# Mask and row maximum in two wide VectorE steps, and a first piece of the MLP set among the attention blocks

## Chip, cores and metric

The kernel runs on one core of a Trainium2 chip. The metric is device time in microseconds. Engines are named as in the profile: PE is TensorE's matmul (PEld its weight load), DVE is VectorE, ACT is ScalarE, POOL is GpSimd, SP is SyncE, which issues most of the DMAs.

## What is computed

Windowed softmax attention, a Fourier mixing with a layer norm and an MLP, and a gated MLP, chained, for 4 batches of 576 tokens with 8 heads of 64 (512 features):

```
rel = pos[:, None] - pos[None, :]
scores = where((rel >= 0) & (rel < 64), q @ k.T / 8, -1e9)
x = softmax(scores) @ v                      # [4, 576, 512]
u = x + real(fft(fft(x, axis=1), axis=2))
u = u + relu(layernorm(u) @ w_ch1) @ w_ch2   # hidden width 2048
h = gelu_tanh(u @ w_in);  a, v = split(h)
v = w_sg @ (layernorm(v) * g_ln) + b_sg      # along the tokens
out = u + (a * v) @ w_out
```

## The kernel before

**Order of the work.** `emit` writes the program as generators that `drive` interleaves: a main generator yields costs, and each lane beside it is advanced by as much. A scheduler then fixes, by its own model, in which order each engine takes the instructions; that order is static on the chip. The stages are the attention, the MLP over 2048 hidden columns, the gated MLP. Beside the attention run lane `weights` (decoding of the weights of FF tiles 0 to 2, `decode`, L144 to L161) and lane `work` (`dft` and `ln` of chunk 0 and of chunk 1).

**Attention.** 36 blocks n (batch b, 64 queries j). `scores` (L254) multiplies the block's queries with 128 keys for four pairs of heads into one PSUM tile `sc` of 4 x 128 columns. For each pair one VectorE step `tensor_tensor_reduce` (L264; in the trace CUSTOM_DVE_ANT_0 and a DVE_READ_ACCUMULATOR2_ANT behind it) adds the mask, writes `s` and the row maximum `mx`; ScalarE takes the exponential of the four pairs (L268). `transposes` (L272) transposes `s` over PSUM tile `pt` into `pts`, `pv` (L281) multiplies with the values, `norm` (L293) divides, `xt` (L312) transposes the result over PSUM tile `xt` into `uT`, which holds all tokens with features on partitions. They follow their block by 1, 2 and 3 blocks (`LAG`). `load_attn` issues the loads of block n + 4 on SP: q in a ring of three, k in three buffers (three blocks each), v in three buffers (two blocks each). The Fourier tables come in four DMAs on POOL's queue, written at blocks 2, 4, 7 and 9 (`TAB_AT`, L376); nothing in them waits for a block. The mask is loaded behind block 0's q and k (L327).

**Fourier step.** `dft(b)` (L380) folds `uT` of a batch: O on GpSimd (L389), E on VectorE (L390), both folded on VectorE (L393, L405), split into high and low parts; a one-row sum `gr`/`grow` on VectorE (L401, L402, L404). Then products with the tables. `ln(n)` (L487) normalises a chunk of tokens into `xh[n]` and `xl[n]`.

**MLP.** A batch's tokens are two chunks of 320 and 256, eight in all; HEAD is chunks 0 to 3, TAIL 4 to 7. `PHASES` lists which FF tiles f go over which chunks, in order. For each (f, chunk): 12 products into `h` (4 x `mm3`, three products each for high and low parts), relu on ScalarE (`rh`, L568), rest on VectorE (`rl`, L569), two tiles later 12 products into `acc` (`second`, L535); behind the last tile of a phase four VectorE adds bring `acc` into `uT` (L549). Beside it run `rest` (decoding of tile 3, `ln` of chunks 2 and 3 with `dft(2)`, `dft(3)`, `ln` of TAIL) and further decodings.

## Time and profile before

| | |
|---|---|
| runs shown | 816.88 us median of 3 (815.56 to 817.01) |
| the profiled execution | 811.93 us |
| its span (first to last instruction) | 810.2 us |
| busy: PE, PEld, DVE, ACT, POOL | 777.8, 748.4, 478.2, 290.9, 163.5 us |
| chain that ended last, by engine | PE 74%, DVE 14%, DMA 6%, ACT 2%, issue 2% |

PE and PEld overlap, and a matmul's end in the trace is modelled, so start-to-start times tell more of TensorE's pace than durations do. In the chain, "DMA" is a wait for a transfer and "issue" time in which the engine waited for nothing that is shown.

### The profile page before, as it was taken

What the parts mean: (1) busy time and instruction counts of PE and PEld (TensorE: products, weight loads), DVE (VectorE), ACT (ScalarE), POOL (GpSimd) and SP (SyncE); (2) the same over time, 40 slices, a digit from 0 to 9 for tenths busy, and PEclk for the clock granted to TensorE, in tenths of its full rate; (3) what the DMA queues carried; (4) which work ended last, traced back from release to release, by engine and by line L of the source; (5) the groups of instructions that cost most, each with busy time, mean ns of one, the idle gap of its engine ahead of it and who ended that gap; (6) DMA issues with size and microseconds to landing.
All of it is one profiled execution on the core that took longest, in us unless ns stands there. A gap on an engine that the chain in (4) does not pass through costs nothing.

```text
span 810.2 us, 15611 instructions
## 1 busy us (share of the span) xinstructions
PE 777.8 (96%) x6084; PEld 748.4 (92%) x6084; DVE 478.2 (59%) x1390; ACT 290.9 (36%) x710; POOL 163.5 (20%) x202
## 2 busy tenths in 40 slices
PE   5979798899999999999999999999999999999998
PEld 5779597899998999999999999999999998989898
DVE  2688978996488557963226933643240258565653
ACT  3777776442233234431113411333242243131310
POOL 1143513442031013410002300232260021010100
PEclk8999999999999999999999999999999999999999
DMA  9997631121012003420002400132140020303032
GB/s 208 295 323 224 177 97 38 61 97 53 2 40 66 1 1 105 129 82 1 1 2 69 136 6 1 34 118 85 40 134 12 0 60 1 117 1 118 1 117 93
DMA packets 59321, 63.70 MB, mean 79 GB/s; under 512 B 22384, under 2 KB 42736, under 8 KB 59248
## 3 DMA queue, kind: packets, MB, share of 16 engines
q1 hardware_dynamic: 58672, 59.75, 24.9%
q0 software_dynamic: 576, 2.97, 1.2%
q8 instruction: 48, 0.79, 0.4%
q14 instruction: 25, 0.20, 0.1%
HBM read 53.25 MB, written 9.44 MB: 77 GB/s over the span
## 4 chain that ended last, share of the span: by engine, by line
PE 74%; DVE 14%; DMA 6%; ACT 2%; issue 2%; SPq 1%; POOL 1%; DVEq 0%; ACTq 0%
PE acc L118 7%; PE acc L119 7%; PE acc L120 7%; PE h L119 6%; PE h L120 6%; PE h L118 6%; PE c L119 6%; PE c L118 6%; PE c L120 6%; PE g L118 3%; PE g L119 3%; PE g L120 3%; DMA dec_s<-in_w 2%; PE sc L260 2%; DMA dec_s<-in_wo 2%
## 5 line engine op out<-in xcount | busy, mean ns | idle before, releaser
L118 PE MATMUL acc<-rh,set 128*128 128x256 f32 (+1 forms) x512 | 151.6, 296 | 2.2 <-DVE uT L549 2.1
L118 PE MATMUL h<-xh,set 128*128 128x256 f32 (+1 forms) x512 | 151.2, 296 | 0.8 <-DVE rl L569 0.8
L119 PE MATMUL acc<-rl,set 128*128 128x256 f32 (+1 forms) x512 | 151.3, 296 | 0.0
L120 PE MATMUL acc<-rh,set 128*128 128x256 f32 (+1 forms) x512 | 151.1, 295 | 0.0
L119 PE MATMUL h<-xl,set 128*128 128x256 f32 (+1 forms) x512 | 151.0, 295 | 0.0
L120 PE MATMUL h<-xh,set 128*128 128x256 f32 (+1 forms) x512 | 150.9, 295 | 0.0
L569 DVE SCALAR_TENSOR_TENSOR rl<-h,rh 128x320 fp32r<-128x320 f32 (+1 forms) x128 | 58.1, 454 | 118.1 <-ACT rh L568 117.6
L160 POOL TENSOR_TENSOR set<-dec_w,set 128x256 fp32r<-128x256 f32 x88 | 71.9, 823 | 253.7 <-ACT set L159 250.4
L568 ACT ACTIVATE rh<-h 128x320 fp32r<-128x320 f32 (+1 forms) x128 | 51.7, 404 | 161.2 <-PE h L120 121.3
L118 PEld LDWEIGHTS acc<-rh,set 128*128 128x128 f32 x512 | 96.4, 188 | 3.6 <-issue 1.3
L118 PEld LDWEIGHTS h<-xh,set 128*128 128x128 f32 x512 | 96.3, 188 | 1.7 <-DVE rl L569 1.3
L120 PEld LDWEIGHTS acc<-rh,set 128*128 128x128 f32 x512 | 96.5, 188 | 0.1
L119 PEld LDWEIGHTS h<-xl,set 128*128 128x128 f32 x512 | 96.4, 188 | 0.1
L120 PEld LDWEIGHTS h<-xh,set 128*128 128x128 f32 x512 | 96.4, 188 | 0.0
L119 PEld LDWEIGHTS acc<-rl,set 128*128 128x128 f32 x512 | 96.4, 188 | 0.0
L549 DVE TENSOR_TENSOR uT<-acc,uT 128x320 f32<-128x320 f32 (+1 forms) x160 | 62.0, 448 | 15.2 <-PE acc L120 15.2
L154 ACT ACTIVATE dec_g<-dec_s 128x256 f32<-128x256 f32 x88 | 38.4, 438 | 78.6 <-DVE dec_w L156 37.0
L268 ACT ACTIVATE s<-s,mx 128x128 f32<-128x128 f32 x144 | 46.9, 393 | 26.4 <-DVE mx L264 26.3
L482 POOL TENSOR_TENSOR rq<-rq,mhalf 128x1 f32<-128x1 f32 (+2 forms) x26 | 17.4, 669 | 189.9 <-DVE rq L481 186.8
L155 DVE TENSOR_SCALAR dec_w<-dec_s 128x256 int32<-128x256 int32 x88 | 34.8, 398 | 35.3 <-POOL set L160 23.1
L120 PE MATMUL c<-xh,set 128*128 128x256 f32 (+1 forms) x188 | 55.4, 294 | 0.0
L118 PE MATMUL c<-xh,set 128*128 128x256 f32 (+1 forms) x188 | 55.3, 294 | 0.0
(190 smaller groups left out, 1611.9 us busy)
## 6 DMA issues: line engine op xcount, KB each, us to landing
dec_s<-in_w SPq DMA_DIRECT2D x64, 256.0 KB, 2.8
v<-in_v SPq DMA_DIRECT2D x16, 520.0 KB, 6.0
k<-in_k SPq DMA_DIRECT2D x11, 512.0 KB, 6.5
dec_s<-in_wi SPq DMA_DIRECT2D x16, 256.0 KB, 2.8
q<-in_q SPq DMA_DIRECT2D x30, 128.0 KB, 5.4
x<-uT SPq DMA_DIRECT2D x4, 640.0 KB, 3.9
out<-uT SPq DMA_DIRECT2D x4, 640.0 KB, 3.9
dec_s<-in_wo SPq DMA_DIRECT2D x8, 256.0 KB, 2.5
```

Of the source, the lines that this page charges most:

```text
L118: mm(out, lhsT=lh, rhs=rh, start=first and i == 0, stop=False)
L119: mm(out, lhsT=lh, rhs=rl, start=False, stop=False)
L120: mm(out, lhsT=ll, rhs=rh, start=False, stop=last and i == n - 1)
L154: nc.scalar.activation(out=g, in_=s[:, :, 1].bitcast(F32), func=AF.Copy, scale=2.0 ** -112)
L155: nc.vector.tensor_scalar(out=w, in0=s[:, :, 0], scalar1=29, scalar2=None, op0=ALU.logical_shift_right)
L160: (eng or nc.gpsimd).tensor_tensor(out=lo[:, o:o + 256], in0=f, in1=hi[:, o:o + 256], op=ALU.subtract)
L260: nc.tensor.matmul(sc[:, hp], lhsT=q[:, hp].rearrange("p a b -> p (a b)"), rhs=k[:, hp, o:o + 128], start=True, stop=True)
L268: nc.scalar.activation(out=s[:, hp], in_=s[:, hp], func=AF.Exp, bias=mx[:, hp:hp + 1], scale=-1.0)
L482: self.nc.gpsimd.tensor_tensor(out=y, in0=v, in1=self.mhalf[:m, 0:n], op=ALU.pow)
L549: V.tensor_tensor(out=x, in0=acc[:, c, 0:size], in1=x, op=ALU.add)
L568: A.activation(out=rh, in_=o, func=AF.Relu)
L569: V.scalar_tensor_tensor(out=rl, in0=o, scalar=0.0, in1=rh, op0=ALU.max, op1=ALU.subtract)
```

## The change

- `scores`: one `scalar_tensor_tensor` over 512 columns scales and masks, one `tensor_reduce` over the same 512 takes four negated maxima.
- `sc`, `pt` and `xt` share one PSUM ring of three (before: two, one and one); the bank left over is the new tile `e`.
- `dft`: O goes to VectorE behind E; the three `gr`/`grow` steps go to GpSimd.
- `load_tables` first copies four columns of the last block's `mx` into the table's place on GpSimd, so that each table DMA waits for its block. The mask is loaded between the two halves of the first k.
- k and v have two buffers each; v is loaded one block later (`VL` 3).
- `early`: hidden tiles 0 to 2 of chunk 0 (320 rows) and their way into `uT` as a lane beside the attention, once `ln(0)` and the decoding of tiles 0 to 2 have been written. Chunk 0 later takes tiles 3 to 5 behind chunks 1 to 3.

```diff
+E0 = range(3)
-PHASES = [(range(P0), HEAD), (range(P0, 6), HEAD), (range(P0), TAIL), (range(P0, 6), TAIL),
+PHASES = [(range(P0), HEAD[1:]), (range(3, 6), HEAD[:1]), (range(P0, 6), HEAD[1:]), (range(P0), TAIL), (range(P0, 6), TAIL),
-VL = 2
+VL = 3
-UB, SB, QB, VB = 3, 3, 3, 3
+UB, SB, QB, VB = 3, 3, 3, 2
@@ load_k
-        t = self.ap_.tile([128, 4, 256], F32, tag="k", bufs=3, name="k")
+        t = self.ap_.tile([128, 4, 256], F32, tag="k", bufs=2, name="k")
             self.nc.sync.dma_start(t[:, :, c], self.aps["k"][b, :, :, o + c.start:o + c.stop])
+            if b == g == c.start == 0:
+                self.nc.sync.dma_start(self.mask, self.aps["mask"])
@@ scores
-            sc = ps.tile([128, 4, 128], F32, tag="sc", bufs=2, name="sc")
+            sc = ps.tile([128, 4, 128], F32, tag="ab", bufs=3, name="sc")
+            nc.vector.scalar_tensor_tensor(
+                out=s, in0=sc, scalar=0.125, in1=self.mask[:, int(j == 0)].unsqueeze(1).to_broadcast([128, 4, 128]),
+                op0=ALU.mult, op1=ALU.add)
+            nc.vector.tensor_reduce(out=mx, in_=s, axis=AX.X, op=ALU.max, negate=True)
             for hp in range(4):
-                nc.vector.tensor_tensor_reduce(
-                    out=s[:, hp], in0=sc[:, hp], in1=self.mask[:, int(j == 0)], scale=-0.125, scalar=3e38,
-                    op0=ALU.add, op1=ALU.min, accum_out=mx[:, hp:hp + 1])
-            for hp in range(4):
-                nc.scalar.activation(out=s[:, hp], in_=s[:, hp], func=AF.Exp, bias=mx[:, hp:hp + 1], scale=-1.0)
-            st[n] = s
+                nc.scalar.activation(out=s[:, hp], in_=s[:, hp], func=AF.Exp, bias=mx[:, hp:hp + 1])
+            st[n], st['mx'] = s, mx
@@ transposes, xt
-            pt = ps.tile([128, 4, 128], F32, tag="pt", bufs=1 + XPT, name="pt")
+            pt = ps.tile([128, 4, 128], F32, tag="ab", bufs=3, name="pt")
...
+            t = ps.tile([128, 4, 128], F32, tag="ab", bufs=3, name="xt")
@@ load_tables
+        self.nc.gpsimd.tensor_copy(self.tab[:, c.start:c.start + 4], after[:, 0:4])
         self.tc.keep_in_program_order(self.nc.gpsimd.dma_start(self.tab[:, c], self.aps["tab"][:, c]))
@@ dft
-        G.tensor_tensor(out=O, in0=x[:, 0:2], in1=x[:, 2:4], op=ALU.subtract)
         EF.tensor_tensor(out=E, in0=x[:, 0:2], in1=x[:, 2:4], op=ALU.add)
+        EF.tensor_tensor(out=O, in0=x[:, 0:2], in1=x[:, 2:4], op=ALU.subtract)
...
-        V.tensor_copy(gr[:, 0:1], O[0:1, 0, 0:1])
-        V.tensor_tensor(out=gr[:, 1:289], in0=O[0:1, 0, 1:289], in1=O[0:1, 0, 575:287:-1], op=ALU.add)
+        G.tensor_copy(gr[:, 0:1], O[0:1, 0, 0:1])
+        G.tensor_tensor(out=gr[:, 1:289], in0=O[0:1, 0, 1:289], in1=O[0:1, 0, 575:287:-1], op=ALU.add)
...
-        V.tensor_tensor(out=self.grow[32:33, 0:289], in0=gr[:, 0:289], in1=self.grow[0:1, 0:289], op=ALU.subtract)
+        G.tensor_tensor(out=self.grow[32:33, 0:289], in0=gr[:, 0:289], in1=self.grow[0:1, 0:289], op=ALU.subtract)
+    def early(self, n, fs):
...
+        for f in fs:
+            t = self.sets[f % 8]
+            o = ps.tile([128, 512], F32, tag="e", name="e")[:, 0:size]
+            self.mm3(o, [(t[:, 0, 128 * k:128 * k + 128], t[:, 1, 128 * k:128 * k + 128], xh[:, k], xl[:, k]) for k in range(4)])
...
+            nc.scalar.activation(out=rh, in_=o, func=AF.Relu)
+            nc.vector.scalar_tensor_tensor(out=rl, in0=o, scalar=0.0, in1=rh, op0=ALU.max, op1=ALU.subtract)
+            hid[f] = rh, rl
+            yield EC * size
+        for c in range(4):
+            s = slice(128 * c, 128 * c + 128)
+            o = ps.tile([128, 512], F32, tag="e", name="e")[:, 0:size]
+            self.mm3(o, [(self.sets[f % 8][:, 2, s], self.sets[f % 8][:, 3, s], *hid[f]) for f in fs])
+            x = self.uT[:, c, start:start + size]
+            nc.vector.tensor_tensor(out=x, in0=o, in1=x, op=ALU.add)
+            yield EC * size
@@ emit
+        def early():
+            yield from when(k.early(0, E0), lambda: have >= {0, "w"})
-        fill = [[weights()], [work()]]
+        fill = [[weights()], [work()], [early()]]
```

SP's queue at the start of the program, before:

```order
L216 DMA q_95<-in_q 64x4x64 x2
L208 DMA k<-in_k 128x4x128 x2
L327 DMA mask<-in_mask 128x256
L216 DMA q_95<-in_q 64x4x64 x2
L216 DMA q_96<-in_q 64x8x64 x2
L233 DMA v<-in_v 128x2x520
```

and in the change:

```order
L220 DMA q_95<-in_q 64x4x64 x2
L210 DMA k<-in_k 128x4x128
L212 DMA mask<-in_mask 128x256
L210 DMA k<-in_k 128x4x128
L220 DMA q_95<-in_q 64x4x64 x2
L220 DMA q_96<-in_q 64x8x64 x2
L210 DMA k<-in_k 128x4x256
```

The mask has moved ahead of one k, the first v behind the next k.

TensorE's queue in the attention, just behind the layer norm of chunk 0, before:

```order
L120 MATMUL g<-tab,el 128x258
L275 MATMUL pt<-ident,s 128x128 x4
L260 MATMUL sc<-k,q_96 128x128 x4
L317 MATMUL xt<-ident,x 128x128 x2
L288 MATMUL pv<-v,pts 64x65 x7
```

and in the change (set_69 holds FF tile 0, xh_110 and xl_111 chunk 0):

```order
L279 MATMUL pt<-ident,s 128x128 x2
L292 MATMUL pv<-v,pts 64x65
L264 MATMUL sc<-k,q_95 128x128
L279 MATMUL pt<-ident,s 128x128
L264 MATMUL sc<-k,q_95 128x128 x3
L120 MATMUL e<-xh_110,set_69 128x320
L279 MATMUL pt<-ident,s 128x128
L121 MATMUL e<-xl_111,set_69 128x320
L122 MATMUL e<-xh_110,set_69 128x320
```

Before, only blocks and the `g<-tab` products of `dft(1)` stand there; now `early`'s products do too. The last of the 72 products stands ahead of the last three blocks' scores.

TensorE's queue where the attention ends, before:

```order
L517 MATMUL g<-ident,u 128x128 x8
L317 MATMUL xt<-ident,x 128x64 x4
L500 MATMUL g<-ident,uT 128x128 x4
L118 MATMUL h<-xh_110,set_69 128x320
L119 MATMUL h<-xl_111,set_69 128x320
L120 MATMUL h<-xh_110,set_69 128x320
```

and in the change (xh_112 and xl_113 are chunk 1):

```order
L526 MATMUL g<-ident,u 128x128 x8
L321 MATMUL xt<-ident,x 128x64 x4
L509 MATMUL g<-ident,uT 128x128 x4
L120 MATMUL h<-xh_112,set_69 128x256
L120 MATMUL h<-xh_112,set_70 128x256
L509 MATMUL g<-ident,uT 128x128 x4
L121 MATMUL h<-xl_113,set_69 128x256
```

The MLP now begins with chunk 1; chunk 0's 96 products of tiles 0 to 3 no longer stand ahead of it.

## Rows read from the trace of the kernel before

**Rows 1.** Busy time by stage: length, then busy us (instructions), clock, DMA share, GB/s.
```profile
11.20:40.00 28.80, 25.21 (x271) 22.48 (x272) 16.24 (x107) 20.64 (x60) 3.20 (x7) 0.93 1.04 280
40.00:147.80 107.80, 93.35 (x1012) 81.84 (x1012) 91.39 (x356) 73.84 (x201) 40.72 (x49) 1.00 0.57 168
147.80:177.80 30.00, 29.02 (x217) 27.74 (x215) 28.79 (x69) 15.33 (x42) 12.86 (x12) 1.00 0.23 72
...
260.00:600.00 340.00, 338.65 (x2554) 336.98 (x2553) 172.50 (x422) 99.66 (x236) 59.78 (x63) 1.00 0.16 52
```
**Rows 2.** The chain of waits before 40 us: start, us, what.
```profile
2.89 0.63 SPq L208
3.56 7.53 DMA mask<-in_mask
```
**Rows 3.** Busy time, the attention behind 80 us in two parts (PE, PEld, DVE, ACT, POOL).
```profile
80.00:105.00 25.00, 19.63 (x212) 15.84 (x210) 21.94 (x87) 17.64 (x47) 11.93 (x10) 1.00 0.61 168
105.00:147.80 42.80, 38.01 (x416) 33.17 (x415) 34.97 (x124) 25.95 (x67) 12.09 (x18) 1.00 0.24 71
```
**Rows 4.** VectorE's first block in the timeline.
```profile
11.24 0.29 DVE L264 CUSTOM_DVE_ANT_0 s<-sc,mask 128x128 f32<-128x128 f32 x1 [8.76 <-DMA mask<-in_mask]
...
12.09 0.08 DVE L264 DVE_READ_ACCUMULATOR2_ANT mx<- 128x1 f32 x1
```
**Rows 5.** VectorE, 512-wide steps: a group before 148 us, then two timeline rows.
```profile
L504 DVE BATCH_NORM_STATS2 st<-u 128x6 f32<-128x512 f32 x4 | 2.6, 665 | 0.7 <-ACT u L502 0.7
...
27.41 0.69 DVE L307 TENSOR_TENSOR x<-pv,rd 128x512 f32<-128x512 f32 x1
28.02 0.28 DVE L155 TENSOR_SCALAR dec_w<-dec_s 128x256 int32<-128x256 int32 x1
```
**Rows 6.** Busy time of line L264 alone, by stage.
```profile
40.00:105.00 65.00, 15.98 (x136) 1.00 0.78 232
105.00:147.80 42.80, 7.73 (x64) 1.00 0.24 71
```
**Rows 7.** Timelines of VectorE and GpSimd: E of batches 0 to 2, O of batch 0.
```profile
46.77 3.04 DVE L390 TENSOR_TENSOR E<-uT 128x1152 f32<-128x1152 f32 x1
45.95 2.65 POOL L389 TENSOR_TENSOR O<-uT 128x1152 f32<-128x1152 f32 x1 [2.55 <-ACT uT L319]
86.60 2.23 DVE L390 TENSOR_TENSOR E<-uT 128x1152 f32<-128x1152 f32 x1
119.05 3.54 DVE L390 TENSOR_TENSOR E<-uT 128x1152 f32<-128x1152 f32 x1
```
**Rows 8.** VectorE's g-row steps before 148 us, groups.
```profile
L404 DVE TENSOR_TENSOR grow<-gr,grow 1x289 fp32r<-1x289 f32 x3 | 2.9, 976 | 0.1
L402 DVE TENSOR_TENSOR gr<-O 1x288 f32<-1x288 f32 x3 | 1.3, 437 | 0.0
```
**Rows 9.** TensorE's timeline: first MLP products, and chunk 2's first.
```profile
147.88 0.39 PE L118 MATMUL h<-xh,set 128*128 128x320 f32 x1
149.87 0.31 PE L119 MATMUL h<-xl,set 128*128 128x320 f32 x1
179.92 0.31 PE L118 MATMUL h<-xh,set 128*128 128x320 f32 x1
```
**Rows 10.** VectorE's timeline: the last part of chunk 0's layer norm.
```profile
107.01 0.42 DVE L520 TENSOR_TENSOR xl<-g,xh 128x256 fp32r<-128x256 f32 x1
```
**Rows 11.** VectorE's timeline: chunk 0's four adds, the last part of chunk 2's layer norm.
```profile
174.75 1.68 DVE L549 TENSOR_TENSOR uT<-acc,uT 128x320 f32<-128x320 f32 x4
177.34 0.41 DVE L520 TENSOR_TENSOR xl<-g,xh 128x256 fp32r<-128x256 f32 x1
```
**Rows 12.** DMA issues before 60 us: count, KB each, us to landing.
```profile
tab<-in_tab POOLq DMA_DIRECT2D x2, 870.0 KB, 5.6
tab<-in_tab POOLq DMA_DIRECT2D x2, 578.5 KB, 8.3
...
k<-in_k SPq DMA_DIRECT2D x2, 256.0 KB, 3.2
```

More of the change, by code (lines that the diff above doesn't have):

```diff
@@ L33 @@
 NV = 0
-VL = 2
-LAG, XPT = (1, 2, 3), 0
+VL = 3
+LAG = 1, 2, 3
 PACE = 1.0
+EC = 5
 FP = ()
-UB, SB, QB, VB = 3, 3, 3, 3
+UB, SB, QB, VB = 3, 3, 3, 2
 WARM, W0, W1 = 16, 9000, 2500
@@ L314, in xt @@
             i = j // 2
-            t = ps.tile([128, 4, 128], F32, tag="pt", bufs=2, name="xt") if XPT else ps.tile([128, 4, 128], F32, tag="xt", name="xt")
+            t = ps.tile([128, 4, 128], F32, tag="ab", bufs=3, name="xt")
             for c in range(4):
@@ L326, in attention @@
             nc.tensor.transpose(warm[:, 0:128], self.ident, self.ident)
-        nc.sync.dma_start(self.mask, self.aps["mask"])
         for n in range(1, 4):
@@ L332, in attention @@
             if n in TAB_AT:
-                self.load_tables(TAB_AT.index(n))
+                tab_at = TAB_AT.index(n)
+            else:
+                tab_at = None
             if n < N:
                 scores(n)
+            if tab_at is not None:
+                self.load_tables(tab_at, st["mx"])
             self.load_attn(n + 4)
@@ L373, in open_dft, with load_tables @@
                 nc.gpsimd.memset(u[:].bitcast(F32), 0.0)
-    def load_tables(self, i):
+    def load_tables(self, i, after):
         w = 2 * (516 + 512) + 258
         c = slice(*((0, w // 2), (w // 2, w), (w, w + 1740), (w + 1740, w + 3480))[i])
+        self.nc.gpsimd.tensor_copy(self.tab[:, c.start:c.start + 4], after[:, 0:4])
         self.tc.keep_in_program_order(self.nc.gpsimd.dma_start(self.tab[:, c], self.aps["tab"][:, c]))
@@ L527, in open_mlp @@
         self.mlp_es.enter_context(es)
+    def early(self, n, fs):
+        nc, p, ps = self.nc, self.ap_, self.aps_
+        start, size = CHUNKS[n]
+        xh, xl = self.xh[n], self.xl[n]
+        hid = {}
+        for f in fs:
+            t = self.sets[f % 8]
+            o = ps.tile([128, 512], F32, tag="e", name="e")[:, 0:size]
+            self.mm3(o, [(t[:, 0, 128 * k:128 * k + 128], t[:, 1, 128 * k:128 * k + 128], xh[:, k], xl[:, k]) for k in range(4)])
+            rh = p.tile([128, CA], F32R, tag="erh", bufs=len(fs), name="erh")[:, 0:size]
+            rl = p.tile([128, CA], F32R, tag="erl", bufs=len(fs), name="erl")[:, 0:size]
+            nc.scalar.activation(out=rh, in_=o, func=AF.Relu)
[9 more added lines that the diff above has]
+            yield EC * size
     def mlp(self, before):
@@ L765, in scaled @@
                 yield w * PACE
+        have = set()
         def work():
@@ L770, in work @@
                 yield from scaled(k.ln(b))
+                have.add(b)
         def weights():
@@ L856, in before @@
                 drain(lanes[1])
-                if g == 3:
+                if g == 4:
                     lanes[1].append(decodes((8, 9), 2000))
-                elif g == 4:
+                elif g == 5:
                     drain(lanes[0])
                     lanes[1].append(decodes(range(10, 13), 7000))
-                elif g == 5:
+                elif g == 6:
                     lanes[1].append(decodes(range(13, 16), 5000))
-                elif g == 6:
+                elif g == 7:
                     lanes[1].append(w_in())
```

1 line of the change is left out of this document (added).

## The prediction

> **What bounds the kernel now.** I read the busy time by stage first [rows 1]. After 260 us TensorE is busy 338.65 of 340.00 us: whatever the change saves must come from less TensorE time left over for that part, or from an earlier start of it. The first 260 us are where TensorE has holes: it starts late, is idle 3.6 us from 11.2 to 40 and 14.5 us from 40 to 147.8 (the attention with the transform and layer norm of batch 0 and part of batch 1's beside it), and 1.0 us in the first 30 us of the MLP. In the attention no one engine is full: VectorE is busy 91.39 of 107.80 us there, TensorE 93.35.
>
> The chain of waits says what ends last at the start: the transfer of the mask, issued at 3.56 us and 7.53 us in flight [rows 2]; up to 40 us the DMA engines' share is 1.04 [rows 1]. From 40 us it alternates, so I split that stage [rows 3]: from 80 to 105 VectorE is busy 21.94 of 25 us, with TensorE at 19.63; from 105 to 147.8 TensorE is busy 38.01 of 42.8, VectorE 34.97. The granted clock is 1.00 from 40 us on, which is the 2.4 GHz level, so no term below is a clock term.
>
> **The masked maximum: more VectorE time, not less.** Now a block of scores costs four 128-wide steps, each with a read of its accumulator. The first starts at 11.24 and the fourth's read at 12.09 [rows 4], so a block holds VectorE for about 0.85 us, 0.21 for each step. The changed kernel has one 512-wide step from PSUM and one 512-wide maximum from SBUF. No such rows exist yet; the nearest are the 512-wide product from PSUM, 0.69 us, with the next instruction 0.61 us behind its start (27.41 to 28.02), and the 512-wide statistics, 0.665 us [rows 5]. Two steps at about 0.60 us are 1.21 us, 0.36 more per block; if the maximum has to wait for the end of the first step, 0.69 + 0.665 = 1.35 us, 0.50 more. Eleven of the 36 blocks lie before 40 us, 17 from there to 105 us, 8 after (136 and 64 instructions there, eight a block) [rows 6]. So +4.0 us before 40 us, under the 12.6 us that VectorE is idle there [rows 1], costs nothing while the transfers bound that stage; +9.0 us after it (bounds 9.0 and 12.5).
>
> Here the Trainium skill speaks the other way: "VectorE: DVE Perf Modes", section on the TRN2 errata, says that an operand in SBUF costs a fixed extra time per instruction and advises steps of 512 elements or more to pay it once. By that rule eight instructions turned into two would be a saving. The trace does not bear it out for this operation: the 128-wide steps follow each other in 0.21 us, so four of them cost less than two 512-wide ones [rows 4, 5]. I go by the rows and keep the rule as a rival.
>
> **E and O on VectorE, the g row on GpSimd.** In the trace E waits for GpSimd's O: E begins 0.82 us after O and ends 1.2 us after O does (46.77 + 3.04 against 45.95 + 2.65) [rows 7]. So E alone is about 1.25 us. Three E in the attention take 3.04 + 2.23 + 3.54 = 8.8 us; six E and O would take 7.5. The two larger g-row steps that leave VectorE took 1.3 and 2.9 us [rows 8]. Together 5.5 us less (8.8 + 4.2 - 7.5); the same steps on GpSimd can hold two-input VectorE steps back as O did, by up to all of it. I take -4.0 us (bounds -5.5 and 0).
>
> **FF tiles 0 to 2 of 320 rows.** That is 36 products into the hidden tile and 36 out of it. At 320 columns they start 0.147 us apart (147.88 to 149.87 is 13 steps with one slower first) [rows 9], so 72 x 0.147 = 10.6 us of TensorE that leave the MLP and enter the attention. They need the layer norm of batch 0's first 320 rows, which is there only at 107.4 us [rows 10]; the order puts them beside the last blocks. VectorE gets three 320-wide steps and four adds, 0.42 us each (four adds take 1.68) [rows 11]: +2.9 us. From 105 to 147.8 TensorE is idle 4.8 us [rows 3], so of 10.6 at least 5.8 lengthen that stretch: **+5.8 us**. VectorE is idle 7.8 us there, and gains 2.9 + 8 blocks x 0.36 - one transform's 1.3 = 4.5: that fits. Before 105, VectorE gains 17 x 0.36 = 6.1 and loses 2.7, +3.4 into 8.6 us of idle: taken as nothing, with the whole 3.4 as its upper bound. The shared PSUM ring of three for scores and both transposes takes the place of four banks; where a transposition lies between two blocks, the scores wait for the mask step before. I cost that at nothing since VectorE's queue ends last there anyway; at most 0.6 us x 18 pairs.
>
> **The start.** The mask is issued one DMA earlier (2.89, where the second k is now, instead of 3.56) and no table is in front. A transfer of the first keys landed in 3.2 us, the mask in 7.5 [rows 2, 12], so the first masked step comes at about 6.3 us instead of 11.24: 4.9 us. The first table, 578.5 KB, now goes behind block 2; the other three follow blocks 4, 7 and 9, so the bytes come back before 40 us. VL = 3 and two buffers for keys and values mean that a load is queued later on SP, behind q loads and weight tiles that wait for their rings. I keep 4.0 of 4.9 us (bounds 0 and 4.9): **-4.0 us**. The Trainium skill has a rule against this move ("SBUF — State Buffer", on transfers started from GpSimd's queue: a busy VectorE keeps their descriptors from being written). In the trace it costs nothing visible: of the four table transfers the two small ones, one of them issued while VectorE was idle, took 8.3 us and the two large ones 5.6 [rows 12].
>
> **The MLP behind it.** Chunk 0 no longer stands first, so TensorE reaches chunk 2 earlier. Now chunk 2's first product is at 179.92, 32.0 us after the MLP's first [rows 9]; its layer norm is ready at 177.75 [rows 11], 29.9 us after, VectorE being busy 28.79 of 30 us [rows 1]. The change takes chunk 0's four relu steps and four adds (3.3), the wait for O (2.3) and the g row (0.9) out of that stretch and adds O (1.2): ready after about 24.6 us. TensorE has only 32.0 - 1.1 idle - 96 x 0.147 = 16.8 us of work until then. So chunk 2 starts 24.6 us behind the attention, 7.4 sooner, and chunk 0's tile 3 (24 x 0.147 = 3.5 us) is still owed: **-3.9 us**, of 10.6 taken out. Bounds: -10.6 if VectorE keeps up, 0 if the weight tiles, which the order puts among these steps, hold GpSimd and VectorE as they did before.
>
> **Sum.** -4.0 + 5.8 - 3.9 = -2.1 us. The profiled execution took 811.93 us (span 810.2), 4.95 under the median of the runs shown, 816.88; against it the sum gives 809.8, against the median 814.8. A measurement of this kernel can tell about 0.2%, 1.6 us, from no change.
>
> **Rivals.** *The attention takes it in.* TensorE's and VectorE's holes from 40 to 147.8, 14.5 and 16.4 us, are larger than what is added (10.6 and 7.9). If the new order fills them, the 5.8 goes to nothing or 1, and VectorE's rows behind the attention, relieved, let chunk 2 start two us sooner: -10, 806.9. Against it: the products can't start before 107 us.
>
> *VectorE becomes the bound* (the other side). 25 x 0.50 + 2.9, and nothing back from E and O, is 15.4 us on an engine already busy 85% of the stage, each block waiting for mask and maximum in series. It decides once fewer than 9.6 of the 16.4 idle us can be used (15.4 - 9.6 is TensorE's 5.8). If only 1.5 can, the attention ends 13.9 - 4.0 = 9.9 us later instead of 1.8, and the sum is +6.0: 822.9. For it: from 80 to 105 VectorE is 88% busy, TensorE 79% [rows 3].
>
> *Two long steps are cheap.* If mask and maximum together take 0.85 us or less, VectorE loses 9.0 us less in the attention; if two thirds of that are time, the sum is -8: 808.9. Against it stand the rows of 512-wide steps, each over 0.6 us [rows 5]. The Trainium skill's rule on fixed costs, named above, would make this case the likely one.
>
> *The change does not do it.* The order could set the products where TensorE is not idle at all, so that they stand in the attention and not beside it: -4.0 + 10.6 - 3.9 = +2.7, 819.6. For it: from 105 us TensorE is busy 89% already [rows 3].
>
> **Numbers.** Forecast 0.40 (own range 810 to 819, which the bounds of the start and of the MLP term give: 0.9 of the 4.9 us more and 4 us of MLP more, or nothing kept of the start; 0.24 faster, 0.11 within 0.2%, 0.05 slower), taken in 0.22, VectorE-bound 0.27, cheap steps 0.05, no hiding 0.06 (half of it within 0.2%). Faster 0.24 + 0.22 + 0.05 = 0.51; same 0.11 + 0.03 = 0.14; slower 0.05 + 0.27 + 0.03 = 0.35. The range reaches from a fuller first rival, -14 (803), to the second's price, 823.
>
> **What would show it.** First masked step near 6.3 us; mask and maximum at 0.65 to 0.7 us each; the three E without a wait; hidden tile e between about 105 and 140 us; the MLP's first product near 149.7 with chunk 2's about 24.6 us behind it, and TensorE waiting on VectorE's layer norm in between. I am wrong if the attention ends before 145 or after 155 us, if chunk 2 does not wait, or if a load of keys or values stops TensorE for several us.

## The result and the profile after

The changed kernel takes 819.55 us (median of 14 runs, 816.35 to 820.96); the kernel before, run beside it, takes 814.25 (14 runs, 812.96 to 817.01). The ratio is 1.0058, 95% interval 1.0045 to 1.0070: 4.7 us slower by the ratio, where 2.1 us faster was forecast. The profiled execution of the changed kernel took 819.26 us with a span of 817.5, 7.3 us more than the span of before. A profile is one execution: that of the kernel before (811.93 us) is 1.0 us under the best of its 98 other runs here and 2.3 under the median of these 14, so some 2 of the 7.3 us are chance.

The start came as forecast, and so did the durations. The timelines of VectorE and ScalarE, first block (start us, us, engine, line, operation, output from inputs; in brackets the idle time before it and who ended it):

```profile
6.99 0.69 DVE L267 SCALAR_TENSOR_TENSOR s<-sc,mask 128x512 f32<-128x512 f32 x1 [4.51 <-PE sc L264]
7.72 0.69 DVE L270 TENSOR_REDUCE mx<-s 128x4 f32<-128x512 f32 x1
8.44 1.28 ACT L272 ACTIVATE s<-s,mx 128x128 f32<-128x128 f32 x4 [6.43 <-DVE mx L270]
```

The first masked step begins at 6.99 us instead of 11.24 [rows 4]. It now waits for the scores, not for the mask, which landed in 3.1 us. Mask and maximum hold VectorE for 1.4 us, against 0.85. What the sum of the forecast left out is in the third row: the first exp begins 1.45 us behind the first masked step. In the kernel before it began 0.33 us behind it (11.57 against 11.24), since a quarter of the maximum was enough. All four exps are done 2.7 us behind the first masked step, where it was 1.6.

The places where E begins mark the end of each batch's attention. VectorE's timeline, E of batches 0 to 3:

```profile
43.41 1.35 DVE L398 TENSOR_TENSOR E<-uT 128x1152 f32<-128x1152 f32 x1
...
90.62 1.31 DVE L398 TENSOR_TENSOR E<-uT 128x1152 f32<-128x1152 f32 x1
...
128.90 1.35 DVE L398 TENSOR_TENSOR E<-uT 128x1152 f32<-128x1152 f32 x1
...
163.71 1.35 DVE L398 TENSOR_TENSOR E<-uT 128x1152 f32<-128x1152 f32 x1
```

Before, these were at 46.77, 86.60, 119.05 [rows 7] and 147.93. So the change is 3.4 us ahead after batch 0, 4.0 us behind after batch 1, 9.9 behind after batch 2 and 15.8 behind after batch 3. Batches 2 and 3 hold the FF products, 36 from 115.3 us on and 36 from 131.0: at the 0.147 us of [rows 9] 5.3 us each, about the 5.9 that each of the two batches loses. The 7.4 us of batch 1 were not in the forecast.

Busy time by stage (length, then busy us of PE, PEld, DVE, ACT, POOL, the granted clock, DMA share, GB/s), which answers to [rows 1, 3]:

```profile
11.20:40.00 28.80, 24.58 (x262) 20.92 (x261) 19.40 (x42) 20.45 (x56) 6.65 (x15) 0.92 1.10 281
40.00:105.00 65.00, 53.77 (x545) 46.90 (x542) 55.45 (x115) 43.81 (x119) 22.71 (x32) 0.95 0.76 201
105.00:147.80 42.80, 42.29 (x388) 38.37 (x387) 28.64 (x57) 22.89 (x61) 6.95 (x12) 1.00 0.35 92
...
177.80:260.00 82.20, 76.57 (x571) 74.45 (x572) 64.55 (x157) 31.42 (x79) 25.00 (x32) 0.98 0.18 58
260.00:600.00 340.00, 339.29 (x2562) 338.00 (x2561) 174.43 (x431) 98.28 (x233) 59.78 (x63) 1.00 0.16 51
```

From 105 us TensorE is full, as forecast. From 40 to 105 TensorE and VectorE are both less busy than before (55.34 and 56.42 there), and the clock is 0.95 instead of 1.00. From 177.8 to 260 TensorE has lost 4.2 us (80.74 before): most of it the forecast wait for chunk 2's layer norm (3.7 us in the two stops ahead of chunk 2's first product).

The timelines of TensorE and VectorE behind the attention: the MLP's first product, the last step of that layer norm on VectorE, the stop, chunk 2's first product:

```profile
163.66 0.48 PE L120 MATMUL h<-xh,set 128*128 128x256 f32 x2
179.50 1.45 DVE L520 TENSOR_SCALAR u<-u,mv,rs 128x512 f32<-128x512 f32 x3
180.10 0.47 PE L526 MATMUL g<-ident,u 128*128 128x128 f32 x1 [2.43 <-DVE u L520]
187.84 0.46 PE L120 MATMUL h<-xh,set 128*128 128x320 f32 x2
```

Chunk 2 starts 24.2 us behind the first product; 24.6 was forecast. In between TensorE is busy 20.2 us, where the forecast gave it 16.8 us of work. From the MLP's first product to its end the kernel takes 653.8 us instead of 662.3, 8.5 less.

Where the 7.4 us of batch 1 went is seen in TensorE's long stops. Its timeline, the row behind each stop of over 1.9 us between 10 and 105 us, and one row of scores at full speed (40.91):

```profile
22.47 0.43 PE L321 MATMUL xt<-ident,x 128*128 128x128 f32 x2 [2.69 <-DVE x L311]
...
40.91 1.06 PE L264 MATMUL sc<-k,q 128*128 128x128 f32 x8
...
46.54 1.98 PE L264 MATMUL sc<-k,q 128*128 128x128 f32 x8 [3.62 <-DMA k<-in_k]
...
79.33 1.21 PE L279 MATMUL pt<-ident,s 128*128 128x128 f32 x4 [2.10 <-ACT s L272]
...
98.92 0.33 PE L279 MATMUL pt<-ident,s 128*128 128x128 f32 x1 [1.98 <-ACT s L272]
```

And the clock there, in stretches of 4 us:

```profile
20.00:24.00 4.00, 1.53 (x9) 1.56 (x10) 1.76 (x5) 2.39 (x7) 1.59 (x3) 0.84 1.11 300
24.00:28.00 4.00, 4.00 (x46) 3.37 (x46) 2.02 (x6) 2.12 (x6) 0.02 (x1) 0.73 1.17 334
...
44.00:48.00 4.00, 1.46 (x7) 1.49 (x8) 2.02 (x2) 0.86 (x3) 0.93 (x2) 0.83 1.07 276
48.00:52.00 4.00, 3.72 (x47) 3.41 (x46) 3.11 (x6) 1.77 (x4) 0.33 (x1) 0.75 1.04 272
...
80.00:84.00 4.00, 3.55 (x23) 2.48 (x24) 3.42 (x8) 3.21 (x10) 2.65 (x4) 0.59 0.26 49
...
100.00:104.00 4.00, 3.71 (x32) 2.69 (x32) 3.11 (x9) 3.66 (x11) 1.10 (x2) 1.00 0.43 162
...
180.00:184.00 4.00, 3.90 (x22) 3.90 (x22) 3.49 (x11) 1.67 (x4) 0.00 (x0) 0.61 0.07 25
```

In this trace each stop of 2.1 us or more, the one at 180 too, is followed by 3 to 4 us at 0.50, the 1.2 GHz level, in which eight score products take 1.98 us instead of 1.06. Behind the stop at 79.33 the clock fell only some 1.4 us after TensorE had begun again, during a second stop of 0.45 us. Behind the stop of 1.98 us at 98.92 it stayed at 1.00. In the profiled execution of the kernel before, whose longest stop between 13 and 260 us is 1.77, it did not fall from 40 us on. The Trainium skill ("TensorE: Matmul & The Clock Gate", Part 1) says that throttled is the state of rest and that activity lifts it; the rows agree. What stood ahead of three of the stops is in the chain of waits:

```profile
13.96 6.84 DMA dec_s<-in_w
...
33.35 13.05 DMA k<-in_k
...
71.90 6.57 DMA dec_s<-in_w
```

A key load took 13.05 us. It shares the time with tables 3 and 4 (870 KB each, issued at 33.46 and 37.59; before, at 34.86 and 54.67). Two weight tiles were nearly 7 us under way, and behind their decode steps VectorE and ScalarE had the x of the norm, the maximum and the exps in their queues.

An account of the two traces: in stretches of 4 us up to 300 us I sum what TensorE is not busy (idle), and its busy time times one minus the clock (clock). Before: idle 27.4, clock 1.7. After: 26.8 and 6.9. Of the 7.3 us between the spans, idle gives -0.6 and the clock +5.2; 2.7 is in neither and stays unexplained. So 10.6 us of products moved into the attention, yet TensorE's idle time did not shrink: holes were filled and others opened.

The +5.2 us of clock is a difference between these two executions, and only a small part of it one between the two kernels. The trace of before has a mean granted clock of 0.996; the 84 runs of that kernel beside the experiments have 0.986 to 0.994, with a median of 0.9905. The changed kernel's 14 runs have 0.983 to 0.991, with a median of 0.990. By these medians the clock makes some 0.4 us of difference (an estimate: 0.0005 of 815 us, each clock being rounded to 0.001). And three kernels below lose 4.8, 7.8 and 8.6 us to the clock in this account and are faster than before. So the clock does not explain why the change is slower.

### The profile page after: what moved, and what is told of

It reads as the page before. It is cut to its first block, busy times and chain, and to the rows that moved or that the text cites. A ratio compares the mean times of both kernels' runs of the same rounds, so it can differ in the third digit from the quotient of the medians.

```text
span 817.5 us, 15421 instructions
## 1 busy us (share of the span) xinstructions
PE 786.8 (96%) x6084; PEld 755.3 (92%) x6084; DVE 487.0 (60%) x1166; ACT 294.7 (36%) x710; POOL 157.6 (19%) x214
## 4 chain that ended last, share of the span: by engine, by line
PE 80%; DVE 7%; DMA 6%; ACT 2%; issue 2%; POOL 1%; SPq 1%; DVEq 0%; ACTq 0%; POOLq 0%
PE acc L120 7%; PE acc L121 7%; PE acc L122 7%; PE h L122 7%; PE h L121 7%; PE h L120 7%; PE c L121 6%; PE c L120 6%; PE c L122 6%; PE g L122 3%; PE g L120 3%; PE g L121 3%; PE sc L264 3%; PE pv L292 2%; DMA dec_s<-in_wo 2%; DMA dec_s<-in_w 2%
## 5 line engine op out<-in xcount | busy, mean ns | idle before, releaser
L120 PE MATMUL acc<-rh,set 128*128 128x256 f32 (+1 forms) x500 | 148.1, 296 | 0.5 <-DVE uT L582 0.5
L121 PE MATMUL acc<-rl,set 128*128 128x256 f32 (+1 forms) x500 | 147.6, 295 | 0.0
L122 PE MATMUL acc<-rh,set 128*128 128x256 f32 (+1 forms) x500 | 147.5, 295 | 0.0
L121 PE MATMUL h<-xl,set 128*128 128x256 f32 (+1 forms) x500 | 147.3, 295 | 0.0
L120 PE MATMUL h<-xh,set 128*128 128x256 f32 (+1 forms) x500 | 146.9, 295 | 0.2 <-DVE rl L602 0.2
L122 PE MATMUL h<-xh,set 128*128 128x256 f32 (+1 forms) x500 | 147.0, 294 | 0.0
L602 DVE SCALAR_TENSOR_TENSOR rl<-h,rh 128x256 fp32r<-128x256 f32 (+1 forms) x125 | 56.6, 453 | 121.3 <-ACT rh L601 120.9
L601 ACT ACTIVATE rh<-h 128x256 fp32r<-128x256 f32 (+1 forms) x125 | 50.4, 404 | 168.2 <-PE h L122 119.4
L120 PEld LDWEIGHTS acc<-rh,set 128*128 128x128 f32 x500 | 94.5, 189 | 1.0 <-issue 0.9
L120 PEld LDWEIGHTS h<-xh,set 128*128 128x128 f32 x500 | 93.9, 188 | 0.6 <-DVE rl L602 0.5
L122 PEld LDWEIGHTS acc<-rh,set 128*128 128x128 f32 x500 | 94.3, 189 | 0.1
L122 PEld LDWEIGHTS h<-xh,set 128*128 128x128 f32 x500 | 94.2, 188 | 0.0
L582 DVE TENSOR_TENSOR uT<-acc,uT 128x256 f32<-128x256 f32 (+1 forms) x156 | 60.4, 448 | 13.5 <-PE acc L122 13.4
L121 PE MATMUL c<-xl,set 128*128 128x256 f32 (+1 forms) x188 | 55.3, 294 | 0.0
```

What stands on the lines that cost most here:

```text
L120: mm(out, lhsT=lh, rhs=rh, start=first and i == 0, stop=False)
L121: mm(out, lhsT=lh, rhs=rl, start=False, stop=False)
L122: mm(out, lhsT=ll, rhs=rh, start=False, stop=last and i == n - 1)
L582: V.tensor_tensor(out=x, in0=acc[:, c, 0:size], in1=x, op=ALU.add)
L601: A.activation(out=rh, in_=o, func=AF.Relu)
L602: V.scalar_tensor_tensor(out=rl, in0=o, scalar=0.0, in1=rh, op0=ALU.max, op1=ALU.subtract)
```

## The experiments

Every kernel was run beside the kernel before; a price in us is (ratio - 1) x 815. Three theories stood at the outset. L: loads that come late stop TensorE, through the tables, the two buffers, or both. P: the FF products stand on top of a TensorE that is already full. M: the longer masked maximum holds VectorE. The runs are told here by what they are part of, not in the order in which they were made; R, F, G, S, C and W are named in the expectations where they come up.

**Putting the change together, one part at a time.** The order is start, E/O, maximum, ring, two buffers, FF products.

Start alone, on the kernel before (the mask's DMA and the four table loads as in the changed kernel):

```diff
+            if b == g == c.start == 0:
+                self.nc.sync.dma_start(self.mask, self.aps["mask"])
...
+                self.load_tables(tab_at, st['mx'])
```

> The kernel before with the mask behind the first keys and the tables behind blocks 2, 4, 7 and 9, alone. As the prediction has it: first masked step at 6.3 to 7 us instead of 11.24, 3 to 4 us faster than before. Rival L (the start is given back before 40 us by loads of keys, values, queries or weight tiles that now meet the tables): within 1.5 us of before, or slower, with a stop of TensorE of over 2 us on a load between 12 and 50 us and a granted clock of 0.50 behind it.

Measured: 809.61 us, ratio 0.9932 (0.9914 to 0.9949), **-5.5 us**, the fastest kernel of all. First masked step at 7.20. E of batches 0 and 1 in its timeline:

```profile
42.37 1.36 DVE L396 TENSOR_TENSOR E<-uT 128x1152 f32<-128x1152 f32 x1
...
83.96 2.89 DVE L396 TENSOR_TENSOR E<-uT 128x1152 f32<-128x1152 f32 x1
```

It is 4.4 us ahead after batch 0 and 2.6 after batch 1: the bytes of the tables do not take the start back here. The stop that L named is there all the same, 2.45 us on a key load at 14.10 with the clock at 0.50 from there to 20 us. Account: idle 22.3, clock 4.8.

Start and E/O (besides, the lines on O, behind E, and on the g row as in the change):

```diff
-        G.tensor_tensor(out=O, in0=x[:, 0:2], in1=x[:, 2:4], op=ALU.subtract)
+        EF.tensor_tensor(out=O, in0=x[:, 0:2], in1=x[:, 2:4], op=ALU.subtract)
```

> The kernel before with the start (mask behind the first keys, tables behind blocks) and with E and O on VectorE and the g row on GpSimd; old masked maximum, old rings, no FF products. If the two gains add: 804 to 807. If both fill the same stop of TensorE (the one before 60 us): 808 to 811.

Measured: 811.03, 0.9951 (0.9936 to 0.9967), **-4.0 us**. The two gains don't add; beside the start E/O makes 1.5 us of loss, with an uncertainty of some 2. Account: idle 23.5, clock 8.6.

Start, E/O and maximum (the changed kernel without FF products, with three buffers and the old rings):

```diff
-            sc = ps.tile([128, 4, 128], F32, tag="ab", bufs=3, name="sc")
+            sc = ps.tile([128, 4, 128], F32, tag="sc", bufs=2, name="sc")
...
-        t = self.ap_.tile([128, 4, 256], F32, tag="k", bufs=2, name="k")
+        t = self.ap_.tile([128, 4, 256], F32, tag="k", bufs=3, name="k")
```

> The changed kernel without the FF products beside the attention, with three buffers for keys and values, and with the PSUM rings of before: start, masked maximum and E/O remain. By the prices of the parts alone (-6.1 + 2.9 - 4.2): 807 to 810. If the ring of three costs here what it costs alone, that is 8 us or more below the same kernel with the ring (816.5); if it costs only in the order of before, within 3 us of 816.5.

Measured: 814.99, 1.0009 (0.9993 to 1.0024), **+0.7 us**: the maximum alone makes 4.7 us of difference to the run before it. Busy time from 11 to 40 us, first with the old maximum, then with the new:

```profile
11.00:40.00 29.00, 25.25 (x281) 22.34 (x280) 16.02 (x100) 19.91 (x56) 5.85 (x15) 0.94 1.11 332
```

```profile
11.00:40.00 29.00, 21.16 (x243) 18.73 (x242) 17.92 (x36) 18.49 (x53) 5.34 (x13) 0.94 1.00 303
```

TensorE gets 38 products fewer done, at the same clock, and batch 0's E comes at 47.96 instead of 41.18. VectorE is busy only 1.9 us more. The chain of waits of the second shows what stood ahead of its longest stop:

```profile
20.84 12.02 DMA q<-in_q
32.91 3.64 PE sc L264 x16
```

A query load was under way for 12.02 us, beside tables 2 and 3, issued at 19.07 and 25.41. So what this pair of traces shows is again a load beside others, in one execution (817.92 us, where that kernel's median is 814.99). How much of the 4.7 us between the medians comes from such loads, and how much from the two long steps as such, is not shown. By the prices of the parts alone 807 to 810 was expected: those do not add.

The same with the ring of three:

```diff
-            sc = ps.tile([128, 4, 128], F32, tag="sc", bufs=2, name="sc")
+            sc = ps.tile([128, 4, 128], F32, tag="ab", bufs=3, name="sc")
```

> As the run before (no FF products beside the attention), and with three buffers for keys and values again and values loaded two blocks ahead. Theory L, if the two buffers are what makes loads late: 3 us or more below the run before, and no stop of TensorE on a key load. If the tables alone make them late: within 1 us of the run before, with the same stop near 43 us. Theories P and M: within 1 us of the run before.

Measured: 816.48, 1.0020 (1.0004 to 1.0037), **+1.6 us**. The ring costs 0.9 us here, with an uncertainty of some 2: its price alone (below) belongs to the order of before. And this run is 3.8 us below the one that follows, as L expected of the buffers, though a stop of 1.82 us on a key load (at 14.00) is left, of which L expected none. P and M, which expected less than 1 us between the two runs, fail.

The same with two buffers for keys and values (the changed kernel without FF products alone):

```diff
-        fill = [[weights()], [work()], [early()]]
+        fill = [[weights()], [work()]]
```

> The changed kernel without the FF products beside the attention (all FF tiles of all chunks in the MLP, as before); everything else, two buffers for keys and values too, as changed. Theory P: the attention ends 9 to 11 us earlier (MLP's first product at 153 to 155) and the MLP gives 8 to 9 us back: 1 to 3 us less in all. Theory L: as the holes of the attention are left open either way, the first MLP product comes only 4 to 8 us earlier and the whole is the same or slower than the changed kernel (0 to +4 us). Theory M: as L, with VectorE over 85% busy up to 105 us as now.

Measured: 821.02, 1.0066 (1.0039 to 1.0092), **+5.4 us**. The first product of the MLP comes at 155.1, so the FF products lengthen the attention by 8.6 us; the rest takes 664.0 us without them and 653.8 with them, 10.2 back. Net of the FF products: -0.7 us by the ratios, with an uncertainty of some 2.4. P, which expected 1 to 3 us less without the products, fails. L has the whole right and misses the attention by 0.6 us (4 to 8 us shorter was expected, 8.6 measured). M gave the same numbers as L, so this run does not tell those two apart.

**The other parts alone, on the kernel before.**

E/O (O and the g row as in the change):

```diff
-        V.tensor_copy(gr[:, 0:1], O[0:1, 0, 0:1])
+        G.tensor_copy(gr[:, 0:1], O[0:1, 0, 0:1])
```

> The kernel before with E and O both on VectorE and the g row on GpSimd, alone. As the prediction sums it (VectorE 4.0 us less in the attention, 2 us less behind it): 0.5 to 4 us faster than before. Rival G (GpSimd, which now does the g row, el and ol in a row, makes the first product of the transform wait: 1.4 us at 51.67 in the changed kernel): 0 to 3 us slower.

E/O alone: 811.33, 0.9945 (0.9924 to 0.9966), **-4.5 us**, just past the end of what was expected. Account: idle 21.9, clock 7.8.

The masked maximum:

```diff
-                nc.vector.tensor_tensor_reduce(
+            nc.vector.scalar_tensor_tensor(
+            nc.vector.tensor_reduce(out=mx, in_=s, axis=AX.X, op=ALU.max, negate=True)
```

> The kernel before with the two-step masked maximum alone. By the prediction's sum (VectorE 0.36 to 0.50 us more per block, 25 blocks behind 40 us, 9 to 12.5 us on an engine with 16 us to spare): 0 to +5 us against the kernel before. Rival F (run with the old maximum in the changed kernel was 5.7 us slower than the changed kernel, so the two steps help): 1 to 5 us faster than before.

Maximum alone: 818.62, 1.0040 (1.0022 to 1.0057), **+3.3 us**, inside the 0 to 5 us that were expected. Account: idle 31.3, clock 6.4.

Start and maximum together:

```diff
+                self.nc.sync.dma_start(self.mask, self.aps["mask"])
+            nc.vector.tensor_reduce(out=mx, in_=s, axis=AX.X, op=ALU.max, negate=True)
```

> The kernel before with the start and the two-step masked maximum. If the maximum costs by itself (+3.3 alone, +4.7 behind start and E/O): 811 to 815, 3 us or more above the start alone. If E/O was what it collided with: within 1.5 us of the start alone (809.6).

Start and maximum: 820.27, 1.0063 (1.0040 to 1.0086), +5.1 us, 10.7 more than the start alone: more than was expected either way. In all three pairs without FF products and two buffers the kernel with the two long steps is 3 us or more slower. The Trainium skill's advice of long steps ("VectorE: DVE Perf Modes", TRN2 errata), which the prediction weighed, does not settle this case: it is on cutting the same work into short steps, and no run here has the same work both ways. Here the four short steps pass over the 512 columns once, in 0.85 us, and the two long ones twice, at 0.69 us each.

The ring (pt and xt likewise):

```diff
-            sc = ps.tile([128, 4, 128], F32, tag="sc", bufs=2, name="sc")
+            sc = ps.tile([128, 4, 128], F32, tag="ab", bufs=3, name="sc")
```

> The kernel before with one PSUM ring of three for scores and both kinds of transposes, alone. As the prediction costs it (nothing): within 1 us of before. Rival R (the ring ties scores to the transposes before them, makes the stops of TensorE longer and drops the clock): 3 us or more slower, granted clock under 1.00 in several places between 20 and 148 us.

Ring of three alone: 827.89, 1.0155 (1.0134 to 1.0177), **+12.6 us**. Its waits up to 150 us (total, times, longest):

```profile
DVE rc L303 <- PE pv L288: 13.3, 10, 2.2
PE xt L317 <- DVE x L307: 12.3, 5, 5.0
```

Before, the second is 6.1 us with a longest of 1.8. TensorE's queue now holds one block of scores at a time between the transposes, and in front of them an x transpose waits for VectorE. Account: idle 29.7, clock 10.2.

The same with a ring of four:

```diff
+            sc = ps.tile([128, 4, 128], F32, tag="ab", bufs=4, name="sc")
```

> The kernel before with one ring of four tiles for scores and both kinds of transposes, the same four banks as before. Theory R3: within 2 us of before (the ring of three cost 12). Rival RS: 6 us or more slower.

Ring of four alone: 819.62, 1.0059 (1.0042 to 1.0076), +4.8 us, between both theories: most of the ring's price alone is its three tiles, some of it the sharing. By what way the missing fourth tile costs is open: with four, TensorE's queue holds one block of scores at a time too, and it waits 12.0 us for x (longest 6.0).

Two buffers (VB = 2 and VL = 3 likewise):

```diff
-        t = self.ap_.tile([128, 4, 256], F32, tag="k", bufs=3, name="k")
+        t = self.ap_.tile([128, 4, 256], F32, tag="k", bufs=2, name="k")
```

> The kernel before with two buffers for keys and for values (values loaded three blocks ahead), alone. Theory L (loads that are issued later stop TensorE; in the changed kernel without FF products these waits of TensorE on keys, queries and values are 6.5 us with two buffers, 2.5 with three): 2 to 5 us slower, with waits of TensorE on loads that the kernel before does not have behind its start. Rival (they are late only beside tables that come at the same time): within 1.5 us of before.

Two buffers alone: 820.73, 1.0052 (1.0032 to 1.0071), **+4.2 us**, in place +3.8. The price is as theory L has it, the way is not: behind the first blocks TensorE waits for no load there. Account: idle 28.1, clock 12.2. That late loads stand behind its stops is not shown: from 16 to 150 us VectorE and ScalarE wait 5.1 us in all for weight tiles, in the kernel before 6.2.

**Taking parts out of the changed kernel, or moving them.**

Three of the four tables later:

```diff
-TAB_AT = (2, 4, 7, 9)
+TAB_AT = (2, 5, 9, 13)
```

> The changed kernel with the four table loads behind blocks 2, 5, 9 and 13 instead of 2, 4, 7 and 9. Theory L (late loads): in the changed kernel TensorE stands still from 42.9 to 46.5 us because a key load issued at 33.35, between two table loads of 870 KB at 33.46 and 37.59, takes 13.05 us; with the last table later that load lands in 8 us or less, the stop goes, and so does the lower granted clock behind it: 2 to 5 us less than the changed kernel, first product of the MLP at 159 to 162 instead of 163.7. Theory P (the products of FF tiles 0 to 2 stand on top of a full TensorE) and theory M (the longer masked maximum holds VectorE): within 1 us of the changed kernel, since another wait ends last.

Measured: 828.24, 1.0159 (1.0133 to 1.0184), 8.2 us slower than the changed kernel. The stop on keys was gone, as L says, but a value load issued at 39.28 took 9.58 us and stopped TensorE for 3.28 us at 48.91; idle 31.5, clock 12.7. L's remedy failed.

The old masked maximum in the changed kernel:

```diff
-            nc.vector.tensor_reduce(out=mx, in_=s, axis=AX.X, op=ALU.max, negate=True)
+                nc.vector.tensor_tensor_reduce(
```

> The changed kernel with the masked maximum of before (four 128-wide steps with an accumulator, exp with scale -1); all else as changed. Theory M: VectorE gains 25 blocks x 0.5 us and the exps can begin after the first quarter, 3 us or more less. Theory L: within 1.5 us of the changed kernel, the stops on the key load near 43 us and on weight tiles near 20 and 77 us remain. Theory P: within 1 us.

Measured: 825.18, 1.0118 (1.0095 to 1.0141), 4.9 us slower than the changed kernel. All three theories fail here: in the whole change the two steps help (so too in the pair of runs with the old rings, below).

Work for TensorE in its stops:

```diff
+            if n == 3:
+                idle = ps.tile([128, 512], F32, tag="e", name="e")
+                for i in range(20):
+                    nc.tensor.transpose(idle[:, 0:128], pr[:, 3], self.ident)
```

> The changed kernel with idle work for TensorE at the places of its three long stops in the attention (20 transposes into the hidden tile's bank behind block 3's transposes, 28 smaller ones behind block 8's x transposes, 12 products behind the second stage of batch 0's transform); nobody reads what they write. Theory C (each stop of over 2 us is followed by about 4 us at the granted clock 0.50, 2 us of TensorE each): the granted clock stays at 1.00 behind these places, 3 to 6 us less than the changed kernel though 60 instructions are added. Rival W (what costs is the wait itself; the clock behind it is hidden in other waits): 0 to 3 us more than the changed kernel.

Measured: 827.11, 1.0143 (1.0121 to 1.0165), 6.9 us slower than the changed kernel. TensorE's timeline at the first place:

```profile
18.28 2.35 PE L283 MATMUL e<-ident,s 128*128 128x128 f32 x20
20.96 0.41 PE L325 MATMUL xt<-ident,x 128*128 128x128 f32 x2 [0.33 <-DVE x L315]
21.20 1.06 PE L264 MATMUL sc<-k,q 128*128 128x128 f32 x8
```

Here and at the third place (75.41) the stop is filled, the clock stays at 1.00 behind it, and eight score products take 1.06 us where they took 1.90 in the changed kernel (22.71): that stop and clock go together there is shown. At the second place a stop of 3.17 us came ahead of the filling, and the clock fell. The time did not come back: the added rows are some 6.7 us of TensorE, idle stays at 26.5 (clock 5.7), and the first product of the MLP is at 167.1. Both C and W fail: keeping the clock up with work that nobody needs costs more here than it gives.

The rings of before, with the hidden tile of the FF products in the ring of the transform:

```diff
-            o = ps.tile([128, 512], F32, tag="e", name="e")[:, 0:size]
+            o = self.gtile()[:, 0:size]
```

> The changed kernel with the PSUM rings of before (scores two tiles, both kinds of transposes one each); the hidden tile of the FF products beside the attention then comes from the ring that transform and layer norm use. Theory R (the ring of three, 12 us slower alone, is what turned the change over): 8 us or more less than the changed kernel, so faster than before; first product of the MLP at 157 or earlier. Rival S (the ring's price alone was an accident of that order and not of this one): within 3 us of the changed kernel.

Measured: 827.93, 1.0152 (1.0127 to 1.0177), 7.7 us slower than the changed kernel. R and S both fail. The MLP's first product is at 164.1, as in the changed kernel (163.7); from there the kernel takes 659.8 us instead of 653.8. That the hidden tile, now in the transform's ring, does this is argued, not shown, so the run can't clear or convict the ring of three.

The same with the old masked maximum:

```diff
-            nc.vector.tensor_reduce(out=mx, in_=s, axis=AX.X, op=ALU.max, negate=True)
+                nc.vector.tensor_tensor_reduce(
```

> The run of the changed kernel with the PSUM rings of before, and the four-step masked maximum of before as well. If the two steps cost here what they cost alone (3 us): 2 to 4 us less than that run. If they cost only beside other parts: within 1 us of it.

Measured: 831.57 us, 1.0195 (1.0171 to 1.0220), 3.5 us slower than the run before it, against both expectations.

And with O and the g row as before:

```diff
-        EF.tensor_tensor(out=O, in0=x[:, 0:2], in1=x[:, 2:4], op=ALU.subtract)
+        G.tensor_tensor(out=O, in0=x[:, 0:2], in1=x[:, 2:4], op=ALU.subtract)
```

> The run before this with O on GpSimd and the g row on VectorE again: what is left of the change is the start (mask, tables), the FF products of 320 rows beside the attention, and two buffers for keys and values. The start alone gave 809.6. If the FF products give what the prediction says (+5.8 in the attention, -3.9 behind it): 810 to 813. If they fill holes: 803 to 808. If they or the two buffers cost: over 814.

Measured: 839.32 us, 1.0287 (1.0262 to 1.0313), the last of the three cases expected. With the hidden tile in the transform's ring each further part that is undone makes it worse (account: idle 43.9, clock 11.1).

A ring of four with the hidden tile in it (scores and transposes likewise):

```diff
-            o = ps.tile([128, 512], F32, tag="e", name="e")[:, 0:size]
+            o = ps.tile([128, 512], F32, tag="ab", bufs=4, name="e")[:, 0:size]
```

> The changed kernel with one ring of four tiles for scores, transposes and the hidden tile of the FF products, instead of a ring of three and a tile of its own. Theory R3 (scores can't run ahead in a ring of three): 4 us or more less than the changed kernel, since the fourth tile is free until 115 us. Rival RS (sharing a ring in program order is what costs, three or four): within 2 us of the changed kernel.

Measured: 828.45 us, 1.0153 (1.0133 to 1.0172), 7.7 us slower than the changed kernel. In this order a fourth shared bank is no gain over a bank of its own for the hidden tile; both theories fail.

## Why the prediction was wrong, point by point

**Start: right.** -4.0 forecast, -5.5 alone; in the changed kernel 3.4 us of it are still there when batch 0 ends. The Trainium skill's rule that the prediction names there is narrower on its page ("SBUF — State Buffer", on the two separate sides) than the prediction tells it: it is on VectorE steps in certain modes, not on any busy VectorE. No run here tests it; in the changed kernel the four tables landed in 8.3 to 9.3 us.

**E and O: right in size, gone in the sum.** The rows are 1.35 us without a wait, and alone the edit gives 4.5 us. Once the start is in, 1.5 us of loss with 2 of uncertainty is left.

**Masked maximum: right in VectorE's time, wrong in what it costs.** The forecast took +9.0 us of VectorE, set them against its idle time and wrote nothing down. The kernel with it is 3.3 us slower alone and 4.7 in place; in the whole change, beside the FF products, it is 4.9 us faster with it. What it measurably adds and the sum did not count is 1.1 us on the way of a block from its first masked step to its last exp; that this is the price is argued, not shown, since in place the loss stands behind a query load.

**The room for the FF products: priced at nothing.** The ring of three ("I cost that at nothing since VectorE's queue ends last there anyway; at most 0.6 us x 18 pairs") costs 12.6 us alone, past that upper end of 10.8, and 0.9 in place. Two buffers ("a load is queued later on SP") cost 4.2 alone and 3.8 in place.

**FF products: both terms mis-sized, the sum nearly right.** Attention +8.6 instead of +5.8, behind it -10.2 instead of -3.9; -0.7 by the ratios, where +1.9 was forecast. Chunk 2 came to within 0.4 us of its forecast place. What failed behind the attention is the 3.5 us "still owed" from then on: from chunk 2's first product to the end the changed kernel takes 629.7 us, the kernel before 630.3. TensorE had done 3.4 us more in the wait than the 16.8 us that were counted, which fits.

**The step that failed** is to put parts of the change at nothing because VectorE had idle time or ended last anyway: the longer maximum ("+3.4 into 8.6 us of idle: taken as nothing"), the ring of three ("I cost that at nothing"), and the loads that are queued later, which got no term at all. In the order in which the change is put together above they come to 4.7, 0.9 and 3.8 us, 9.4 in all. The whole missed its forecast by 6.8 us (+4.7 against -2.1): these 9.4 and E/O's 1.5, less 1.5 of the start and 2.6 of the FF products, which came out better. The two buffers are the surest of the three, with much the same price alone and in place; the ring's 0.9 is inside its uncertainty, and the maximum's price changes its sign beside the FF products. By what way each of them costs is open.

A premise ahead of the sum was weak too: "The granted clock is 1.00 from 40 us on, ... so no term below is a clock term". It was read from one execution, 4.95 us under the median by the prediction's own words, with a clock that none of the 84 other runs reached. Of the 19 other kernels profiled here none loses less than 2.8 us to the clock up to 300 us, and some lose up to 12.7. But kernels that lose more to it than the changed one are faster than before, so this is not what turned the change over.

Of the prediction's own signs of being wrong two came: the attention ended after 155 us (163.7), and a load of keys stopped TensorE for 3.62 us. The third, that chunk 2 does not wait, did not.

The time landed nearest the rival "VectorE becomes the bound" (+6.0), but by luck and not by its mechanism: from 40 to 105 us VectorE is less busy than before.

**What stays open.** The staircase -5.5, -4.0, +0.7, +1.6, +5.4, +4.7 ends at the whole change and names its parts, but it is one order of several, and a part's price hangs on the others: the five parts alone, without the FF products, sum to +10.1, together they are +5.4, and the maximum changes sign beside the FF products. Each part shifts when loads are issued and what they meet, and several of the longest stops stand behind such loads (keys 13.05 us, queries 12.02, values 9.58, weight tiles 6.84). Others do not, such as the 5.0 us that an x transpose waits for VectorE in the ring of three. Why one order meets them and another doesn't was not settled, nor the 2.7 us that are neither idle nor clock.

## What to carry to other kernels

Where several engines take turns in ending the chain, an edit that is priced at nothing because an engine has idle time is not priced: ask how much longer one unit's way through the engines gets, what each buffer that is given up lets start later, and which loads then meet. A profile is one execution: before writing "no clock term", compare its time and its mean clock with those of other runs of the same kernel. And run each part of a bundle alone: here the start by itself, 809.6 us, beats both kernels.

## What was not expected of the hardware

The length of a stop of TensorE alone does not decide whether the clock falls. In the changed kernel a stop of 2.10 us was followed by the 1.2 GHz level and one of 1.98 was not (79.33 and 98.92), while another of 1.98 at the start was (8.93). Between kernels the lengths even cross. E/O alone, then start, E/O and maximum, each with TensorE's row behind the stop and the next 4 us:

```profile
51.90 0.39 PE L423 MATMUL g<-tab,grow 128*128 128x258 f32 x1 [1.80 <-POOL grow L404]
52.00:56.00 4.00, 4.00 (x25) 2.88 (x25) 3.23 (x16) 3.20 (x11) 3.97 (x5) 0.58 0.64 146
```

```profile
102.75 0.66 PE L279 MATMUL pt<-ident,s 128*128 128x128 f32 x4 [2.25 <-ACT pts L281]
104.00:108.00 4.00, 4.00 (x51) 3.58 (x47) 3.94 (x14) 4.00 (x12) 1.46 (x2) 1.00 0.52 166
```

Behind 1.80 us the clock fell, behind 2.25 it stayed at 1.00.

And a load can take about twice its usual time beside others: 512 KB of keys landed in 13.05 us beside two tables, 128 KB of queries in 12.02, against medians of 7.0 and 6.5 in the first 60 us of the kernel before. That the other loads make it so is inferred from their times.
